# Second-level Strassen for M1 in the later quads of Mixer 2, with VectorE held in program order

## The chip, the core and the metric

The kernel runs on one core of one Trainium2 chip. The metric is device time in microseconds (us), taken over several executions. The four executions of the kernel before that stand beside the change agreed within 0.3 us (574.78 to 575.06).

Engines are named as the profile names them: PE is TensorE, DVE is VectorE, ACT is ScalarE, SP issues the transfers.

## The reference, cut to what matters

```python
h  = x + A(layernorm(x))                        # linear attention; A is not touched here
u  = gelu(einsum("bsd,sf->bdf", layernorm(layernorm(h)), w1) + b1)   # Mixer 1
y  = einsum("bdf,fs->bds", u, w2) + b2          # Mixer 2: 3584 -> 2048, 1024 columns
out = h + transpose(y)                          # residual
```

Only Mixer 2 is changed: a product of `w2` (3584 x 2048) with `u` (3584 x 1024), plus bias and residual `h`.

## The kernel before

Each pair of 128-row blocks of the output (512 columns a half) is one level of Strassen-Winograd: seven products instead of eight. The stationary operand is a block of `w2` or a sum of blocks; the moving operand is a block of `u` or a sum. I call the stationary sums by the number of the product that uses them, S5, S6, S7 and S3, and the moving sums T2, T3 and T4. The products accumulate in tiles A, B and C of PSUM, the memory that matmuls write to:

```python
def asum(self, m):                 # stationary sums, one DVE instruction each
    a, b, op = {
        5: (self.a21, self.a22, ALU.add),
        6: (self.lhs.get(5), self.a11, ALU.subtract),
        7: (self.a11, self.a21, ALU.subtract),
        3: (self.a12, self.lhs.get(6), ALU.subtract),
    }[m]
    t = pools["sa"].tile([P, self.nk, P], FP16, tag="sa", name="sa")[:]   # a pool of 6 buffers
    self.lhs[m] = t
    return nc.vector.tensor_tensor(t, a, b, op)
# p1: A = M1, ACT copies A to B    p6: B += M6, ACT copies B to C    p5: e = M5
# p2: A += M2 -> out(0,0)          p7: C += M7 -> out(1,1) = C + e
# p3: B += M3 -> out(0,1) = B + e  p4: C += M4 (needs T4) -> out(1,0)
```

Two pairs make a quad. In a quad the two M5 products together are again a 2 x 2 block product, and `Inner` does that one with Strassen too: seven products i1 to i7 of 256 columns. Mixer 1 already does so for M1 and M5; Mixer 2 does it for M5 only, in its quads 1, 2 and 3 (quad 0 is plain).

```python
def i1(self):
    ae = psz.tile([P, BANK], F32, tag="z0", bufs=1, name="psI0")
    bc = psz.tile([P, BANK], F32, tag="z1", bufs=1, name="psI1")
    self.a, self.e, self.b, self.c = ae[:, 0:HW], ae[:, HW:CW], bc[:, 0:HW], bc[:, HW:CW]
    self.mm(1, self.a, True)
    nc.scalar.copy(self.b, self.a)
# i6: b += ..., copy b to c   i2: a += ..., sink   i5: e = ..., copy e to SBUF
# i7: c += ..., c + e by DVE  i3: b += ..., b + e by DVE   i4: c += ..., sink
```

The order of a quad, cut to what matters. P4 of a quad runs inside the next quad, and while a quad runs, the next quad's sums are made (`pre`):

```python
for st in self.sts: st.p1()
for st in pend:     st.p4()          # P4 of the quad before, needs T4
on_p4()                              # T3, weight loads
interleave(self.in5, [st.p6 for st in self.sts])
pre(5)                               # next quad's S5 pair and inner sums
for st in self.sts: st.p2()
pre(6)                               # next quad's S6 pair
for st in self.sts: st.p7(...)
on_p7()                              # T4
pre(7)
for st in self.sts: st.p3()
pre(3)
```

The framework orders the instructions of each engine itself, by readiness in a model of the machine, with program order as the priority. An engine then executes its own list in that order.

## Time and profile before

| what | read from | value |
|---|---|---|
| time | median | 574.98 us |
| PE, DVE, ACT busy | page | 99%, 67%, 44% |
| one later quad (quad 2) | timeline of PE | 480.75 to 522.36, 41.61 us |
| 14 matmuls of 512 columns | timeline of PE | 3.02 us, 215.9 ns each |
| 7 matmuls of 256 columns | timeline of PE | 0.763 us, 109.0 ns each |
| DVE busy in such a quad | windows | about 27 of 41 us |

The prediction gives this quad as 480.91 to 522.52; that is the same stretch as the view of the chain places it.

First two lines of the page of the kernel before: busy time of each engine (us, share of the span, instructions), and the chain of work that ended last, by engine.

```profile
PE 566.0 (99%) x3061; PEld 287.2 (50%) x3061; DVE 383.8 (67%) x731; ACT 254.7 (44%) x547; POOL 1.8 (0%) x8
...
PE 93%; DVE 3%; DMA 2%; ACT 2%; issue 1%; SPq 0%; ACTq 0%
```

PE does nearly all of the chain. Next, the timeline of PE in the kernel before, some of quad 2. The columns are the start, the time from the first start to the last end, the engine, the line, the operation, output and inputs, shapes and the count; a bracket at the end would be idle time and what ended it. Busy spans of neighbours overlap (matmuls are pipelined), so lengths are read from start to start.

```profile
480.75 3.18 PE L285 MATMUL psA_5063<-gE,wq 128*128 128x512 f16 x14
483.77 3.19 PE L285 MATMUL psA_5080<-gE,wq 128*128 128x512 f16 x14
486.79 1.67 PE L285 MATMUL psC_4858<-gs_4997,wq 128*128 128x512 f16 x7
...
495.54 0.93 PE L218 MATMUL psI_5142<-gi_4451,is 128*128 128x256 f16 x7
496.31 0.93 PE L218 MATMUL psI_5141<-gE,sa 128*128 128x256 f16 x7
...
522.36 3.18 PE L285 MATMUL psA_5386<-gE,wq 128*128 128x512 f16 x14
```

There is no bracket anywhere in the 41.61 us: PE never waits. The two P1 (`psA`) take 6.04 us and need nothing that was made late, so the P4 behind them (`psC<-gs`, where `gs` holds T4) starts 6.04 us into the quad.

Last, the timeline of DVE of the same kernel at the end of the quad before.

```profile
471.88 1.09 DVE L277 TENSOR_TENSOR sa<-sa,wq 128x1792 f16<-128x1792 f16 x1 [2.27 <-PE psC_4858 L285]
472.89 0.74 DVE L395 SCALAR_TENSOR_TENSOR t_4973<-psC_4858,b_sb,e_4816 128x512 f32<-128x512 f32 x1
473.56 2.02 DVE L1241 TENSOR_TENSOR gs_4997<-gO,gT_4434 128x3584 f16<-128x3584 f16 x1
475.49 1.09 DVE L277 TENSOR_TENSOR sa<-sa,wq 128x1792 f16<-128x1792 f16 x1
```

The first line is the first S6 of the next quad. It waited 2.27 us for a buffer, until the first P7 had consumed its S7 (`psC` is P7's tile). The second S6 (last line) was not free yet, so the scheduler put half of T4 (`gs`) and a P7 eviction before it.

### The profile page before, as it was taken

How to read it: one execution, taken by the hardware profiler on the slowest of the kernel's cores; microseconds unless marked ns; L12 is line 12 of the kernel's file. 1: busy time of each engine (PE TensorE's matmuls, PEld its weight loads, DVE VectorE, ACT ScalarE, POOL GpSimd, SP SyncE). 2: the span in 40 equal slices, each digit the busy share in tenths (PEclk: the TensorE clock that was granted, in tenths of full speed). 3: DMA queues.
4: the chain of work that ended last, by engine and by line, in shares of the span. 5: the costliest groups of instructions: out<-in, count | busy, mean ns of one | idle time of the engine just before them, and what ended most of it. 6: DMA issues, size and time to landing. Idle time of an engine off the chain costs nothing.

```text
span 573.1 us, 8081 instructions
## 1 busy us (share of the span) xinstructions
PE 566.0 (99%) x3061; PEld 287.2 (50%) x3061; DVE 383.8 (67%) x731; ACT 254.7 (44%) x547; POOL 1.8 (0%) x8
## 2 busy tenths in 40 slices
PE   8999999999999999999999999999999999999997
PEld 3444444455555444446555565564444554544544
DVE  6898887556767879863745727442989558557535
ACT  5657777656667776445445354463110100100100
POOL 1000000000000000000000000000000000000000
PEclk9999999999999999999999999999999999999999
DMA  9934432039536762104041240425971852842001
GB/s 309 352 74 83 85 73 38 19 113 318 104 73 130 184 174 102 55 2 146 1 148 55 93 148 1 148 75 146 233 189 47 218 140 67 218 120 73 19 27 47
DMA packets 97798, 66.59 MB, mean 116 GB/s; under 512 B 32082, under 2 KB 91744, under 8 KB 97760
## 3 DMA queue, kind: packets, MB, share of 16 engines
q1 hardware_dynamic: 97024, 65.42, 41.7%
q10 hardware_dynamic: 672, 0.66, 0.3%
q8 instruction: 24, 0.39, 0.3%
q14 instruction: 14, 0.11, 0.1%
q0 software_dynamic: 64, 0.01, 0.0%
HBM read 50.34 MB, written 8.39 MB: 102 GB/s over the span
## 4 chain that ended last, share of the span: by engine, by line
PE 93%; DVE 3%; DMA 2%; ACT 2%; issue 1%; SPq 0%; ACTq 0%
PE acc_t L964 9%; PE acc_t L1112 9%; PE psB L695 4%; PE psC L695 4%; PE psA L695 4%; PE psE L695 2%; PE nd_ps L1063 1%; DMA xr<-in_A_x_dram 1%; PE psB_4758 L285 1%; PE psC_5500 L285 1%; PE psC_5181 L285 1%; PE psB_5064 L285 1%; PE psC_4858 L285 1%; PE psA_4757 L285 1%; PE psC_4527 L285 1%; PE psB_4550 L285 1%
## 5 line engine op out<-in xcount | busy, mean ns | idle before, releaser
L285 PEld LDWEIGHTS <-sa 128*128 128x128 f16 x716 | 70.0, 98 | 77.3 <-issue 0.7
L285 PEld LDWEIGHTS <-wq 128*128 128x128 bf16 x590 | 57.1, 98 | 61.7 <-issue 1.0
L964 PE MATMUL acc_t<-xnT,wq_sb 128*128 128x512 bf16 x256 | 58.0, 379 | 0.0
L1112 PE MATMUL acc_t<-wo_sb,pqT 128*128 128x512 bf16 x256 | 56.1, 379 | 0.0
L277 DVE TENSOR_TENSOR sa<-wq 128x1024 f16<-128x1024 bf16 (+1 forms) x44 | 36.4, 830 | 6.9 <-DMA wq<-in_B_w_dram 2.8
L1112 PEld LDWEIGHTS <-pqT 128*128 128x128 bf16 x256 | 24.8, 98 | 29.0
L964 PEld LDWEIGHTS <-wq_sb 128*128 128x128 bf16 x256 | 24.5, 98 | 27.4
L166 ACT ACTIVATE e_sb<-acc_t 128x512 bf16<-128x512 f32 x40 | 23.9, 597 | 26.5 <-PE acc_t L964 24.3
L170 DVE TENSOR_SCALAR e_sb<-e_sb 128x512 bf16<-128x512 bf16 x64 | 18.5, 289 | 25.4 <-ACT e_sb L166 24.8
L218 PEld LDWEIGHTS <-is 128*128 128x128 f16 x276 | 26.9, 98 | 14.3 <-issue 3.0
L695 PEld LDWEIGHTS <-xs 128*128 128x128 f16 x208 | 20.0, 98 | 23.3 <-DVE xs L681 1.3
L695 PE MATMUL psA<-wkv,xnT 128*128 128x512 bf16 x104 | 26.7, 379 | 0.0
L1123 DVE BATCH_NORM_STATS2 hst<-acc_t 128x6 f32<-128x512 f32 x32 | 22.1, 693 | 6.7 <-ACT h_bf L1122 6.5
L1110 ACT CAST acc_t<-xr 128x512 f32<-128x512 bf16 x32 | 19.0, 593 | 13.4 <-DVE hst L1123 13.3
L695 PEld LDWEIGHTS <-xnT 128*128 128x128 bf16 x156 | 15.3, 98 | 18.5 <-issue 0.2
L167 ACT ACTIVATE r_sb<-acc_t 128x512 bf16<-128x512 f32 x40 | 23.7, 593 | 0.0
L619 PE MATMUL acc_t<-wkv,xnT 128*128 128x512 bf16 x96 | 21.6, 379 | 0.7 <-ACT xnT L872 0.7
L1084 DVE TENSOR_TENSOR o_sb<-nd_ps,rd 128x384 bf16<-128x384 f32 (+1 forms) x48 | 21.7, 504 | 0.6 <-ACT rd L1079 0.4
L588 DVE BATCH_NORM_STATS2 st<-x_sb 128x6 f32<-128x512 bf16 x32 | 20.5, 681 | 1.6 <-DMA x_sb<-in_A_x_dram 1.6
L277 DVE TENSOR_TENSOR sa<-sa,wq 128x1024 f16<-128x1024 f16 (+1 forms) x22 | 18.3, 831 | 3.9 <-PE psC_4858 L285 2.3
L277 DVE TENSOR_TENSOR sa<-wq,sa 128x1024 f16<-128x1024 bf16 (+1 forms) x22 | 18.3, 831 | 3.7 <-PE psI_5141 L218 1.1
L1122 ACT CAST h_bf<-acc_t 128x512 bf16<-128x512 f32 x32 | 18.4, 575 | 1.0 <-PE acc_t L1112 0.9
(722 smaller groups left out, 979.1 us busy)
## 6 DMA issues: line engine op xcount, KB each, us to landing
wq<-in_B_w_dram SPq DMA_DIRECT2D x14, 1024.0 KB, 7.7
wq<-in_B_w_dram SPq DMA_DIRECT2D x8, 1792.0 KB, 10.0
xr<-in_A_x_dram SPq DMA_DIRECT2D x16, 256.0 KB, 3.1
out_dram<-ot SPq DMA_DIRECT2D x31, 128.0 KB, 1.7
x_sb<-in_A_x_dram SPq DMA_DIRECT2D x15, 256.0 KB, 3.2
wkv<-in_A_wqkv_dram SPq DMA_DIRECT2D x2, 1024.0 KB, 9.5
wq_sb<-in_A_wqkv_dram SPq DMA_DIRECT2D x2, 1024.0 KB, 12.7
wo_sb<-in_A_wo_dram SPq DMA_DIRECT2D x2, 1024.0 KB, 6.4
```

The lines of the kernel that those rows point to most:

```text
L166: pin(nc.scalar.activation(e_sb[:], src, ACT.Exp))
L167: pin(nc.scalar.activation(r_sb[:], src, ACT.Relu))
L218: nc.tensor.matmul(ps, lhsT=self.lhs[m][:, k, :], rhs=self.mov[m][:, k, :], start=(start and k == 0), stop=(k == self.nk - 1), skip_group_ ...
L277: return nc.vector.tensor_tensor(t, a, b, op)
L285: nc.tensor.matmul(ps[:, cols], lhsT=lhs[:, k, :], rhs=mv(k)[:, cols], start=(start and k == 0), stop=(k == self.nk - 1), skip_group_check ...
L588: return nc.vector.bn_stats(st[:, c, :], x_sb[:, c * CW:(c + 1) * CW])
L619: mm = nc.tensor.matmul(pp[:, 0:CW], lhsT=xnT[:, kt, i * P:(i + 1) * P], rhs=wkv[:, kt, c * CW:(c + 1) * CW], start=(kt == 0), stop=(kt == ...
L695: pin(nc.tensor.matmul(ps[:], lhsT=lhs[:, k, :], rhs=rhs[:, k, :], start=(start and k == 0), stop=(k == hk2 - 1), skip_group_check=True,))
L964: nc.tensor.matmul(qp[:, 0:SW], lhsT=wq_sb[:, kt, j * P:(j + 1) * P], rhs=xnT[:, kt, u * SW:(u + 1) * SW], start=(kt == 0), stop=(kt == ND ...
L1084: nc.vector.tensor_tensor(o_sb[:, b * JPB * P:(b * JPB + nsl) * P].rearrange("p (s h e) -> p s h e", h=HB, e=DH), blk[:, :, 0:P].rearrange ...
L1112: nc.tensor.matmul(ap_[:, 0:CW], lhsT=pqT[:, j, i * P:(i + 1) * P], rhs=wo_sb[:, j, dc * CW:(dc + 1) * CW], start=(j == 0 and not SEED_RES ...
L1123: nc.vector.bn_stats(st[:, dc, :], ap_[:, 0:CW])
```

## The change

The intent: M1 of quads 1 to 3 of Mixer 2 gets inner Strassen too, as in Mixer 1, which saves 1/8 of its matmul columns. Buffers and moving sums for it need room in SBUF (the on-chip memory of the operands), so the pool of the stationary sums shrinks from 6 to 4 (S7 is now made in place over a block of weights), and evictions move partly to ACT. From quad 1 on every DVE instruction is pinned behind the one traced before it (`dve.held`).

```diff
+    class Dve:
+        held = False
+        def __getattr__(self, name):
+            op = getattr(nc.vector, name)
+            return (lambda *a: pin(op(*a))) if self.held else op
 ... (class Mixer2)
+        def asum(self, m):
+            if m != 7:
+                return super().asum(m)
+            t = self.a21.bitcast(FP16)
+            self.lhs[7] = t
+            return dve.tensor_tensor(t, self.a11, self.a21, ALU.subtract)
 ...
         def out(self, sh, dh, a, b, op):
             op(ot[:, a:b], b2_sb[:, i:i + 1])
+            dve.tensor_tensor(ot[:, a:b], ot[:, a:b], self.hr[sh, dh][:, a:b], ALU.add)
 ...
         def evac(self, sh, dh, ps, a=0, b=CW):
-            self.out(sh, dh, a, b, lambda ot, bias: nc.vector.scalar_tensor_tensor(
-                ot, ps[:, a:b], bias, self.hr[sh, dh][:, a:b], ALU.add, ALU.add))
+            self.out(sh, dh, a, b, lambda ot, bias: nc.scalar.activation(
+                ot, ps[:, a:b], ACT.Identity, bias=bias, scale=1.0))
 ... (class Quad)
+        def begin2(self):
+            self.asums(5)
+            self.in1 = self.inner(1)
+            self.asums(6)
+        def run2(self, pend, nxt, on_p4, on_p7, cut):
+            ...
+            in5 = self.inner(5)
+            self.interleave(self.in1, [st.p4 for st in pend])
+            on_p4()
+            ...                                  # residual loads
+            self.asums(7)
+            self.interleave(in5, [st.p6 for st in sts])
+            self.asums(3)
+            ...                                  # p2, residual loads
+            nxt.begin2()                         # if there is a next quad
+            ...                                  # p7 of both pairs
+            on_p7()                              # T4
+            ...                                  # p3 of both pairs
+            return sts, nxt
 ... (Mixer 2 proper)
-    pools["sa"] = ctx.enter_context(tc.tile_pool(name="sapool2", bufs=6, ...))
+    pools["sa"] = ctx.enter_context(tc.tile_pool(name="sapool2", bufs=4, ...))
-    pools["is"] = inner2
+    pools["is"], pools["is_bufs"] = inner2, 7
+    mov1, sums1 = inner_moving(gE[:, :, 0:CW], NFP, inner2, "gi1")
 ... (end of quad 0)
+    dve.held = True
 ... (also cut: mends of T3, whose input is now overwritten; loads of the residual)
```

More of the change, by code (lines that the diff above doesn't have):

```diff
@@ L198, in inner_moving @@
         return {1: b11, 2: b21, 3: b22, 4: t4, 5: b12, 6: t2, 7: t3}, sums
+    class Dve:
[3 more added lines that the diff above has]
+            return (lambda *a: pin(op(*a))) if self.held else op
+    dve = Dve()
     class Inner:
@@ L208, in sums @@
         def sums(self):
-            sm = [pools["is"].tile([P, self.nk, P], FP16, tag=self.tag, bufs=4, name="is")[:] for _ in range(4)]
-            nc.vector.tensor_tensor(sm[0], self.a21, self.a22, ALU.add)
-            nc.vector.tensor_tensor(sm[1], sm[0], self.a11, ALU.subtract)
-            nc.vector.tensor_tensor(sm[2], self.a11, self.a21, ALU.subtract)
-            nc.vector.tensor_tensor(sm[3], self.a12, sm[1], ALU.subtract)
+            sm = [pools["is"].tile([P, self.nk, P], FP16, tag=self.tag, bufs=pools["is_bufs"], name="is")[:] for _ in range(4)]
+            dve.tensor_tensor(sm[0], self.a21, self.a22, ALU.add)
+            dve.tensor_tensor(sm[1], sm[0], self.a11, ALU.subtract)
+            dve.tensor_tensor(sm[2], self.a11, self.a21, ALU.subtract)
+            dve.tensor_tensor(sm[3], self.a12, sm[1], ALU.subtract)
             self.lhs.update({5: sm[0], 6: sm[1], 7: sm[2], 3: sm[3]})
@@ L276, in asum @@
             self.lhs[m] = t
-            return nc.vector.tensor_tensor(t, a, b, op)
+            return dve.tensor_tensor(t, a, b, op)
         def pre(self, m):
@@ L360, in evac_shared @@
         def evac_shared(self, fh, ps):
-            t = cpool.tile([P, BANK], F32, tag=f"t{fh}", name="t1")
+            t = pools["t"].tile([P, BANK], F32, tag=f"t{fh}", name="t1")
             nc.vector.tensor_tensor(t[:], ps[:], self.e[:], ALU.add)
@@ L371, in __init__, with fetch @@
             super().__init__(p, w2_tiles[p], NFP, gmov)
-        def prefetch(self):
             self.hr = {}
-            for sh in range(2):
-                for dh in range(2):
-                    t = outp.tile([P, CW], BF16, tag=f"hr{self.p % 2}{sh}{dh}", bufs=2 if (sh, dh) == (1, 0) else 1, name="hr")
-                    nc.sync.dma_start(t[:], h_dram[2 * self.p + sh][:, dh * CW:(dh + 1) * CW])
-                    self.hr[sh, dh] = t
+        def asum(self, m):
[4 more added lines that the diff above has]
+            return dve.tensor_tensor(t, self.a11, self.a21, ALU.subtract)
+        def fetch(self, sh, dh):
+            t = outp.tile([P, CW], BF16, tag="hr", bufs=6, name="hr")
+            nc.sync.dma_start(t[:], h_dram[2 * self.p + sh][:, dh * CW:(dh + 1) * CW])
+            self.hr[sh, dh] = t
         def out(self, sh, dh, a, b, op):
@@ L384, in out @@
             op(ot[:, a:b], b2_sb[:, i:i + 1])
+            dve.tensor_tensor(ot[:, a:b], ot[:, a:b], self.hr[sh, dh][:, a:b], ALU.add)
             nc.sync.dma_start(o_dram[i * P:(i + 1) * P, dh * CW + a:dh * CW + b], ot[:, a:b])
         def evac(self, sh, dh, ps, a=0, b=CW):
-            self.out(sh, dh, a, b, lambda ot, bias: nc.vector.scalar_tensor_tensor(
-                ot, ps[:, a:b], bias, self.hr[sh, dh][:, a:b], ALU.add, ALU.add))
+            self.out(sh, dh, a, b, lambda ot, bias: nc.scalar.activation(
+                ot, ps[:, a:b], ACT.Identity, bias=bias, scale=1.0))
         def evac_shared(self, sh, ps):
-            t = cpool.tile([P, BANK], F32, tag=f"t{sh}", name="t2")
-            def op(ot, bias):
-                nc.vector.scalar_tensor_tensor(t[:], ps[:], bias, self.e[:], ALU.add, ALU.add)
-                nc.vector.tensor_tensor(ot, t[:], self.hr[sh, 1][:], ALU.add)
-            self.out(sh, 1, 0, CW, op)
+            self.out(sh, 1, 0, CW, lambda ot, bias: dve.scalar_tensor_tensor(
+                ot, ps[:], bias, self.e[:], ALU.add, ALU.add))
         def done(self):
@@ L420, in sum1 @@
             A, B, c = self.sts[m].A, self.sts[m].B, self.cols(h)
-            nc.vector.tensor_tensor(A[:, c], ps, es, ALU.add)
+            dve.tensor_tensor(A[:, c], ps, es, ALU.add)
             nc.scalar.copy(B[:, c], A[:, c])
@@ L427, in sum5 @@
         def sum5(self, m, h, ps, es):
-            nc.vector.tensor_tensor(self.sts[m].e[:, self.cols(h)], ps, es, ALU.add)
+            dve.tensor_tensor(self.sts[m].e[:, self.cols(h)], ps, es, ALU.add)
         def pre(self, m):
@@ L438, in pre, with interleave, fill @@
                 self.in5.sums()
-        def prefetch(self):
-            for st in self.sts:
-                st.prefetch()
-        def run(self, pend, nxt, on_p4=nop, before_p7=nop, on_p7=nop, cut=None):
-            nk = self.sts[0].nk
-            def interleave(n, fs):
-                steps = [(f, k) for f in fs for k in range(nk)]
-                t = len(steps)
-                cuts = [0, (5 * t + 8) // 16, (9 * t + 8) // 16, (12 * t + 8) // 16, t]
-                def fill(q):
-                    part = steps[cuts[q]:cuts[q + 1]]
-                    for f in fs:
-                        ks = [k for g, k in part if g is f]
-                        if ks:
-                            f(ks)
-                for f in (n.i1, 0, n.i6, n.i2, 1, n.i5, n.i7, 2, n.i3, 3, n.i4):
-                    fill(f) if isinstance(f, int) else f()
+        def interleave(self, n, fs):
+            steps = [(f, k) for f in fs for k in range(self.sts[0].nk)]
+            t = len(steps)
+            cuts = [0, (5 * t + 8) // 16, (9 * t + 8) // 16, (12 * t + 8) // 16, t]
+            def fill(q):
+                part = steps[cuts[q]:cuts[q + 1]]
+                for f in fs:
+                    ks = [k for g, k in part if g is f]
+                    if ks:
+                        f(ks)
+            for f in (n.i1, 0, n.i6, n.i2, 1, n.i5, n.i7, 2, n.i3, 3, n.i4):
+                fill(f) if isinstance(f, int) else f()
@@ new lines, in asums, with inner @@
+        def asums(self, m):
+            for st in self.sts:
+                st.asum(m)
+        def inner(self, m):
+            mov, sink, sink_sum = {
+                1: (self.mov1, self.sink1, self.sum1), 5: (self.mov5, self.sink5, self.sum5),
+            }[m]
+            n = Inner(self.sts, m, mov, "i", sink, sink_sum)
+            n.sums()
+            return n
+        def begin2(self):
[3 more added lines that the diff above has]
+        def run2(self, pend, nxt, on_p4, on_p7, cut):
+            sts = self.sts
+            for st in sts:
+                st.begin()
+            in5 = self.inner(5)
+            self.interleave(self.in1, [st.p4 for st in pend])
+            on_p4()
+            for st in sts:
+                st.shared_tile()
+                st.fetch(0, 0)
+            for sh, dh in ((1, 1), (0, 1)):
+                for st in sts:
+                    st.fetch(sh, dh)
+            self.asums(7)
+            self.interleave(in5, [st.p6 for st in sts])
+            self.asums(3)
+            nxt = nxt()
+            for st in sts:
+                st.p2()
+            for st in sts:
+                st.fetch(1, 0)
+            if nxt is not None:
+                nxt.begin2()
+            for st in sts:
+                st.p7(cut if st is sts[-1] else None)
+            on_p7()
+            for st in sts:
+                st.p3()
+            return sts, nxt
@@ L462, in run @@
+        def run(self, pend, nxt, on_p4=nop, before_p7=nop, on_p7=nop, cut=None):
+            interleave = self.interleave
             if self.mov1 is not None:
@@ L1187 @@
     cpool = ctx.enter_context(tc.tile_pool(name="cpool", bufs=1))
+    pools["t"] = mctx.enter_context(tc.tile_pool(name="tpool", bufs=1, side="right"))
     assert NFP % 2 == 0 and NSP % 2 == 0 and NSP >= 4 and NFP >= 6
     inner1 = mctx.enter_context(tc.tile_pool(name="inner1", bufs=1, side="right"))
-    pools["is"] = inner1
+    pools["is"], pools["is_bufs"] = inner1, 4
     hmov.update(moving(hE, hO, hT2, hT3, hT4))
@@ L1218 @@
     mctx.close()
-    pools["sa"] = ctx.enter_context(tc.tile_pool(name="sapool2", bufs=6, side="right", reuse_waits="tile"))
+    pools["sa"] = ctx.enter_context(tc.tile_pool(name="sapool2", bufs=4, side="right", reuse_waits="tile"))
     w2b = ctx.enter_context(tc.tile_pool(name="w2b", bufs=2, side="right", reuse_waits="tile"))
@@ L1235, with derived @@
     gmov.update(moving(gE, gO, gT2, None, None))
-    def derived(m, of):
+    def derived(m, of, mend=None):
         def make():
@@ L1240, in make, with less_b11 @@
             for h, sl in enumerate(spans):
-                nc.vector.tensor_tensor(ts[h][:], *of(sl), ALU.subtract)
+                dve.tensor_tensor(ts[h][:], *of(sl), ALU.subtract)
+                if mend is not None:
+                    mend(ts[h], sl)
             gmov[m] = lambda k: ts[k // H2][:, k % H2, :]
         return make
-    make_t3 = derived(7, lambda sl: (gT2[:, sl, :], gE[:, sl, 0:CW]))
+    def less_b11(t, sl):
+        k0 = sl.start + sl.start % 2
+        o = t[:, k0 - sl.start:H2:2, HW:CW]
+        dve.tensor_tensor(o, o, gE[:, k0:sl.stop:2, 0:HW], ALU.subtract)
+    make_t3_raw = derived(7, lambda sl: (gT2[:, sl, :], gE[:, sl, 0:CW]))
+    make_t3 = derived(7, lambda sl: (gT2[:, sl, :], gE[:, sl, 0:CW]), less_b11)
     make_t4 = derived(4, lambda sl: (gO[:, sl, 0:CW], gT2[:, sl, :]))
@@ L1249 @@
         load_w2(p, w2b)
+    mov1, sums1 = inner_moving(gE[:, :, 0:CW], NFP, inner2, "gi1")
     mov5, sums5 = inner_moving(gE[:, :, CW:D], NFP, inner2, "gi5")
     def quad2(u):
-        return Quad([Mixer2(2 * u), Mixer2(2 * u + 1)], None, mov5)
+        return Quad([Mixer2(2 * u), Mixer2(2 * u + 1)], mov1, mov5)
     def after_p4(u):
@@ L1265 @@
     for st in pend:
-        st.prefetch()
+        st.fetch(0, 0)
+        st.fetch(1, 1)
+        st.fetch(0, 1)
+    for st in pend:
         if st is pend[1]:
-            for m in (5, 6, 7, 3):
+            for m in (5, 6, 7):
                 st.asum(m)
-            make_t3()
+            make_t3_raw()
         st.p1()
@@ L1274 @@
         st.p6()
+        if st is pend[1]:
+            st.asum(3)
+    sums1()
     sums5()
-    nxt.pre(5)
+    for st in pend:
+        st.fetch(1, 0)
+    nxt.begin2()
     for st in pend:
@@ L1279 @@
     make_t4()
-    nxt.pre(6)
-    nxt.pre(7)
     for st in pend:
         st.p3()
-    nxt.pre(3)
+    dve.held = True
     for u in range(1, NSP // 2):
         cur = nxt
-        cur.prefetch()
         last = 2 * u + 2 == NSP
-        pend, nxt = cur.run(
-            pend, lambda: None if last else quad2(u + 1),
-            on_p4=after_p4(u), on_p7=make_t4, cut=CW - P if last else None,
+        pend, nxt = cur.run2(
+            pend, lambda: None if last else quad2(u + 1), after_p4(u), make_t4, CW - P if last else None,
         )
```

## The prediction

> **What bounds the kernel now.** TensorE. The page gives PE 99% busy, VectorE (DVE) 67%, ScalarE (ACT) 44%; the chain of waits is 93% PE. In Mixer 2 (403 to 570 us) the timeline shows matmul groups back to back: 14 matmuls of 512 columns every 3.02 us (215.9 ns each), 7 of 256 columns every 0.763 us (109.0 ns). That agrees with the Trainium skill ("TensorE: Matmul & The Clock Gate", Back-to-back issue gap: N/2.4 + 2.5 ns). A later quad takes 41.61 us (480.91 to 522.52) with no PE gap. Only fewer matmul columns help.
>
> **Removed.** Inner Strassen replaces 28 x 215.9 ns = 6.05 us of M1 by 49 x 109.0 ns = 5.34 us: 0.71 us per quad, three quads, 2.1 us, all on the critical path.
>
> **Added, off PE.** Per later quad, DVE gets four more inner sums (0.62 us each), two mends of T3 (estimate 0.5 each) and two partial sums (0.42). A residual add with fp32 input took 0.69 us, an all-16-bit one of 512 columns takes 0.42; the fused (0,0) and (1,0) evictions (0.75) move to ACT, leaving a 0.42 add. DVE goes from about 27 to about 30 us of a 41 us quad (estimate). Quad 0 also gets four M1 moving sums (1.09 each); DVE is nearly full there, with slack after 444 us. ACT is nearly idle. Capacity suffices everywhere.
>
> **Moved, where I expect the gain to go.** DVE now runs in program order (the skill's table at the head of the TensorE page lists VectorE's queue as strict FIFO, so a blocked instruction blocks those behind). The sum pool shrinks from 6 to 4. While a quad's S3 pair lives and the next quad's S5 pair is made, all four are taken, so the next quad's S6 pair must wait for P3 of the current quad, its last product. S6 stands in DVE order *before* the P7 evictions and the T4 sums. Before, DVE slipped T4 ahead of a blocked sum; now it cannot. At the end of P3 (time 0) DVE still owes: S6 1.0, two P7 evictions 2.3, T4 2 x 2.0, two P3 evictions 2.3, four in5 sums 2.3, then the first M1 partial sum near 12.7 us (estimate). P4 cannot start before about 5.3.
>
> The scheduler does reorder PE (in Mixer 1 some inner groups swap), so I expect PE to run most of in1 (4.6 us) first, with about 0.5 us exposed behind the ACT copy after i1, and 0.9 us or more before i4, which needs that partial sum: 1.5 to 2.2 us per transition. It happens between quads 1 and 2 and 2 and 3 only (quad 0 is not held, quad 3 has no successor): about 3 to 4.4 us. If PE kept program order, P4 would stall about 4.5 us each time. The last eviction becomes ACT then DVE: about 0.2 us.
>
> **Sum.** 575.0 - 2.1 + 3 + 0.2 = about 576, say 575.9 us; 80% range 572.6 to 580.5. Chances: faster by over 2% 0.01, within 2% 0.97, slower 0.02.
>
> **What would show it.** Inner M1 groups of 7 matmuls at 0.763 us: step 1 right. S6 (128x1792) in DVE's timeline released by P3's psB at the end of quads 1 and 2, the P7 evictions queued after it: blocking right. PE gaps of 0.5 to 5 us at the starts of quads 2 and 3, released by DVE: cost right. No such gaps and a span near 571: wrong.
>
> **What would make it wrong.** The late T4 fully hidden behind in1; an order of PE or ACT that waits on what DVE does last; quad 0's fuller DVE delaying quad 1; late residual or weight loads.

## The result, and the profile after

The changed kernel takes 579.14 us (median of 4 runs, 578.94 to 579.27) against 574.91 us (4 runs) for the kernel before: ratio 1.0069, 95% interval 1.0054 to 1.0084. It is slower by 4.2 us, where its matmul work is 2.1 us less.

The same two lines of the page, of the changed kernel:

```profile
PE 565.5 (98%) x3124; PEld 293.5 (51%) x3124; DVE 390.2 (68%) x759; ACT 272.0 (47%) x585; POOL 1.8 (0%) x8
...
PE 90%; DVE 6%; issue 1%; ACT 1%; DMA 1%; SPq 0%; DVEq 0%; ACTq 0%
```

The shares barely move. What moved is the chain: DVE's part of it doubles from 3% to 6%. The timeline of PE, read from start to start of the quads, says where:

| | before | after | difference |
|---|---|---|---|
| quad 1 | 41.61 (439.14 to 480.75) | 40.92 (439.27 to 480.19) | -0.69 |
| quad 2 | 41.61 (480.75 to 522.36) | 43.61 (480.19 to 523.80) | +2.00 |
| quad 3 | 41.61 (522.36 to 563.97) | 43.61 (523.80 to 567.41) | +2.00 |
| from there to the end of the span | 9.13 (to 573.1) | 9.99 (to 577.4) | +0.86 |

With 0.13 us of difference before quad 1, these sum to the 4.3 us between the spans (573.1 and 577.4). Quad 1 is what the change was made for: 0.69 us gained. Quads 2 and 3 have the same matmuls, so they lose 43.61 - 40.92 = 2.69 us each to waits.

The timeline of PE in the changed kernel around the start of quad 2, beginning with P7 and P3 of quad 1 (`psI` are the inner products, `psC<-gs,wq` from 485.84 is P4). I call the inner products of M1 and M5 together in1 and in5, as the code does:

```profile
468.10 6.21 PE L294 MATMUL psC<-gs,wq 128*128 128x512 f16 x28
474.14 6.21 PE L294 MATMUL psB<-gO,sa 128*128 128x512 f16 x28
480.19 0.93 PE L227 MATMUL psI<-gE,wq 128*128 128x256 f16 x7
481.61 0.93 PE L227 MATMUL psI<-gi,is 128*128 128x256 f16 x7 [0.50 <-ACT psI L237]
482.37 0.93 PE L227 MATMUL psI<-gE,wq 128*128 128x256 f16 x7
483.14 0.60 PE L227 MATMUL psI<-gi,is 128*128 128x256 f16 x4
483.80 0.92 PE L227 MATMUL psI<-gE,is 128*128 128x256 f16 x7
484.56 0.49 PE L227 MATMUL psI<-gi,is 128*128 128x256 f16 x3
485.19 0.81 PE L227 MATMUL psI<-gE,sa 128*128 128x256 f16 x6
485.84 6.21 PE L294 MATMUL psC<-gs,wq 128*128 128x512 f16 x28
491.88 0.27 PE L227 MATMUL psI<-gE,sa 128*128 128x256 f16 x1
492.83 0.93 PE L227 MATMUL psI<-gE,is 128*128 128x256 f16 x7 [0.68 <-DVE psA L205]
494.28 0.92 PE L227 MATMUL psI<-gi,wq 128*128 128x256 f16 x7 [0.52 <-DVE psA L205]
```

In program order P4 is interleaved with i1 to i7. Here the scheduler has run i1, i6, i2, i7 and i5 and even the first product of in5, because P4 was not ready. From start to start, less 109.0 ns a matmul, PE loses 0.66 us before i6, 0.22 before i5, 0.30 before in5's i1, 0.84 before i3 (at 492.83) and 0.69 before i4 (at 494.28), together 2.71. The first three follow ACT copies that P4's matmuls would have covered; the last two follow DVE's M1 partial sums (`psA`).

The timeline of DVE in the changed kernel, same stretch:

```profile
477.37 1.09 DVE L205 TENSOR_TENSOR sa<-sa,wq 128x1792 f16<-128x1792 f16 x1 [3.65 <-PE psB L294]
480.39 1.09 DVE L205 TENSOR_TENSOR sa<-sa,wq 128x1792 f16<-128x1792 f16 x1 [1.93 <-PE psB L294]
481.40 0.74 DVE L205 SCALAR_TENSOR_TENSOR ot<-psC,b_sb,e 128x512 bf16<-128x512 f32 x1
...
483.64 3.95 DVE L205 TENSOR_TENSOR gs<-gO,gT 128x3584 f16<-128x3584 f16 x2
...
491.48 0.62 DVE L205 TENSOR_TENSOR is<-sa,is 128x896 f16<-128x896 f16 x1
...
492.35 0.43 DVE L205 TENSOR_TENSOR psA<-psI,es 128x256 f32<-128x256 f32 x1
493.79 0.43 DVE L205 TENSOR_TENSOR psA<-psI,es 128x256 f32<-128x256 f32 x1 [1.01 <-PE psI L227]
```

The two S6 now wait for `psB`, which is P3, the last product of the quad: 3.65 and 1.93 us of a standing engine. The first P7 eviction stands behind them and starts at 481.40, though both P7 products were complete by 474.31 (468.10 plus 6.21). T4 follows at 483.64, the first M1 partial sum at 492.35, which is 12.2 us after the quad's start. DVE worked 29 us in this quad and still was late with what counted.

The reader should set this beside the same place before: there the second S6 was also blocked, and the scheduler passed it with T4. The change also took cover away. Before, P4 came 6.04 us into the quad, behind P1; now it is to start behind i1, 0.77 us into the quad (s6_last_b below). The first half of T4, late as it is, was ready 5.47 us into quad 2 (483.64 plus 2.02, the time of one half in the kernel before), so by these numbers P1 would still have covered it. That was not run.

### The profile page after: what moved, and what is told of

The parts are those of the page before. It is cut to its first block, busy times and chain, and to the rows that moved or that the text cites. A ratio compares the mean times of both kernels' runs of the same rounds, so it can differ in the third digit from the quotient of the medians.

```text
span 577.4 us, 8298 instructions
## 1 busy us (share of the span) xinstructions
PE 565.5 (98%) x3124; PEld 293.5 (51%) x3124; DVE 390.2 (68%) x759; ACT 272.0 (47%) x585; POOL 1.8 (0%) x8
## 4 chain that ended last, share of the span: by engine, by line
PE 90%; DVE 6%; issue 1%; ACT 1%; DMA 1%; SPq 0%; DVEq 0%; ACTq 0%
PE psB L294 17%; PE psC L294 15%; PE psI L227 11%; PE psA L294 10%; PE acc_t L1016 9%; PE acc_t L1164 9%; PE psB L747 4%; PE psC L747 4%; PE psA L747 4%; PE acc_t L671 2%; PE psE L747 2%; PE psE L294 1%; DVE gs L205 1%; PE nd_ps L1115 1%; DVE ot L205 1%
## 5 line engine op out<-in xcount | busy, mean ns | idle before, releaser
L294 PEld LDWEIGHTS <-wq 128*128 128x128 bf16 (+1 forms) x618 | 59.9, 98 | 63.7 <-issue 1.0
L294 PE MATMUL psC<-gs,wq 128*128 128x512 f16 (+2 forms) x238 | 50.2, 366 | 0.0
L330 ACT COPY psC<-psB 128x512 f32<-128x512 f32 x22 | 12.5, 570 | 35.1 <-PE psB L294 35.1
L294 PE MATMUL psB<-hT,sa 128*128 128x512 f16 x112 | 28.4, 379 | 0.0
L294 PE MATMUL psC<-hT,wq 128*128 128x512 f16 x112 | 28.3, 379 | 0.0
L205 DVE TENSOR_TENSOR ot<-ot,hr 128x512 bf16<-128x512 bf16 (+2 forms) x27 | 11.2, 414 | 24.8 <-ACT ot L403 24.4
L294 PE MATMUL psB<-gT,sa 128*128 128x512 f16 x112 | 26.5, 379 | 0.0
L294 PE MATMUL psA<-hO,wq 128*128 128x512 f16 x112 | 25.6, 379 | 0.7 <-ACT psB L313 0.7
L294 PE MATMUL psB<-hO,sa 128*128 128x512 f16 x112 | 25.5, 379 | 0.0
L294 PE MATMUL psC<-hT,sa 128*128 128x512 f16 x112 | 25.5, 379 | 0.0
```

The costliest lines, as they stand in the source:

```text
L205: return (lambda *a: pin(op(*a))) if self.held else op
L294: nc.tensor.matmul(ps[:, cols], lhsT=lhs[:, k, :], rhs=mv(k)[:, cols], start=(start and k == 0), stop=(k == self.nk - 1), skip_group_check ...
L330: nc.scalar.copy(self.C[:], self.B[:])
```

## The experiments

Theory: the S6 pair has no buffer until P3 is done; it stands in a fixed DVE order before the P7 evictions and T4; so these start 7 us or more late, P4 cannot cover the copies between the inner products, and the M1 partial sums come too late. What DVE still has to do when P3 ends is called the debt below.

Rivals: DVE has simply too much work at the transition; the fixed order as such costs the time; the in5 sums in front of the partial sums are what counts.

| run | edit | median us | ratio to before (95%) |
|---|---|---|---|
| the change | | 579.14 | 1.0069 (1.0054 to 1.0084) |
| s6_last | S6 after the P3 evictions | 573.29 | 0.9977 (0.9962 to 0.9992) |
| s6_last_b | the same, 5 rounds | 573.18 | 0.9969 (0.9957 to 0.9982) |
| s6_mid | S6 after the P7 evictions | 575.23 | 1.0003 (0.9990 to 1.0017) |
| bufs5 | 5 sum buffers, 2 output tiles | 580.18 | 1.0083 (1.0069 to 1.0097) |
| bufs5b | 5 sum buffers, 3 output tiles | 574.96 | 1.0000 (0.9985 to 1.0015) |
| in5_late | in5 sums later | 578.08 | 1.0054 (1.0039 to 1.0069) |
| before_held | the kernel before, DVE held | 575.93 | 1.0025 (1.0008 to 1.0041) |
| unheld | the change, DVE free | 585.49 | 1.0184 (1.0148 to 1.0219) |
| pin_in1 | unheld, only the M1 inner sums pinned | 574.84 | 0.9996 (0.9982 to 1.0009) |
| s6_last_tail | s6_last, last evictions on DVE | 572.93 | 0.9963 (0.9949 to 0.9976) |

### s6_last: the same work, another place in the queue

```diff
 def begin2(self):
     self.asums(5)
     self.in1 = self.inner(1)
-    self.asums(6)
 ... (run2; likewise at the end of quad 0)
     for st in sts:
         st.p3()
+    if nxt is not None:
+        nxt.asums(6)
     return sts, nxt
```

> The changed kernel with one move: the next quad's S6 pair is made after the P3 evictions in VectorE order, no longer before the P7 evictions. Theory (a blocked S6 pair at the head of the in-order VectorE holds up the P7 evictions and T4): the S6 pair still waits for P3, but nothing that TensorE needs soon stands behind it; quads 2 and 3 shrink from 43.61 us to 40.9 each, time about 573.8 us (579.1 minus 2 x 2.7). Rival (VectorE simply has too much work at the transition, or the fixed order as such costs it): the amount of work and the hold are unchanged, so at most 1 us is won and the time stays above 578.

Measured: 573.29 us, and 573.18 in the repeat: 0.5 us below the expected 573.8. The transitions give 2 x 2.7 us back; the rest is probably in the last stores (see s6_last_tail). In the first run one of the four executions, the profiled one, took 575.01: its quads are 40.91 to 40.92 us as well, but it lost 1.7 us in its first 12 us, where PE ran slower. So it was repeated for a clean profile.

> s6_last once more, with five rounds, to set it beside s6_last_tail (572.93) and to take a profile of an execution whose clock was up from the start: 573.2 to 573.4 us, quads of 40.9 us, the last stores landing in 1.6 and 1.5 us.

The timelines of DVE and of PE in s6_last_b, the same place:

```profile
473.55 0.74 DVE L205 SCALAR_TENSOR_TENSOR ot<-psC,b_sb,e 128x512 bf16<-128x512 f32 x1
...
475.79 3.95 DVE L205 TENSOR_TENSOR gs<-gO,gT 128x3584 f16<-128x3584 f16 x2
...
481.90 2.08 DVE L205 TENSOR_TENSOR sa<-sa,wq 128x1792 f16<-128x1792 f16 x2
```

```profile
480.10 0.93 PE L227 MATMUL psI<-gE,wq 128*128 128x256 f16 x7
480.87 2.11 PE L294 MATMUL psC<-gs,wq 128*128 128x512 f16 x9
482.81 0.93 PE L227 MATMUL psI<-gi,is 128*128 128x256 f16 x7
```

T4 is made at 475.79 instead of 483.64, P4 interleaves with the inner products as the program has it, and PE shows no wait at all: quads 1 and 2 start at 439.19 and 480.10, quad 3 at 521.02, 40.9 us each. The number of DVE instructions is the same (759), so "too much work" falls, and so does "the fixed order as such": it is still fixed.

### s6_mid: half the move

```diff
     for st in sts:
         st.p7(cut if st is sts[-1] else None)
+    if nxt is not None:
+        nxt.asums(6)
     on_p7()
```

(and S6 taken out of `begin2`, as above.)

> A half step of the move in s6_last: the S6 pair behind the P7 evictions (2.3 us of VectorE), still before T4 and the P3 evictions. Theory: the debt at the end of P3 is 2.3 us smaller, so the first M1 partial sum comes about 10 us after the quad's start instead of 12.2. TensorE then no longer waits for it (1.5 us of 2.7 gone), but T4 is still late, so i6 still waits for the ACT copy after i1: 1.0 to 1.3 us lost per transition, time 575.5 to 576.5. Rival (only full removal helps, or it is not a queue): near 579 or near 573.3.

Measured: 575.23 us, 0.3 below the range. Quad 2 takes 41.91 us (479.97 to 521.88 in the timeline of PE), so 1.0 us is lost instead of 2.69. The only wait of PE that the profile names is the one of 0.50 us behind the ACT copy, once in each of the two transitions; it names none for the partial sums. A trace of one is left: before i3 PE loses 0.21 us, and i3 starts at 490.37, 0.05 us after the first partial sum ends (489.89 plus 0.43). The loss follows the length of the debt, as a queue should.

### bufs5 and bufs5b: one buffer more, the same order

```diff
-name="sapool2", bufs=4
+name="sapool2", bufs=5
-pools["is"], pools["is_bufs"] = inner2, 7
+pools["is"], pools["is_bufs"] = inner2, 6      # bufs5b: 5
-ot = outp.tile([P, CW], BF16, tag="ot", bufs=3, name="ot")
+ot = outp.tile([P, CW], BF16, tag="ot", bufs=2, name="ot")   # bufs5 only
```

> The changed kernel in its own order, with 5 buffers for the sums instead of 4 (the room comes from 6 inner-sum buffers instead of 7 and 2 output tiles instead of 3). Theory (the missing buffer makes S6 wait for P3): one S6 finds a free buffer, the other needs only the first P3, 3.0 us earlier. So the S6 wait in VectorE is released at P3's first product, T4 is ready some 2.4 us after the quad's start, and 0.5 to 1.2 us are lost per transition instead of 2.7: 574.8 to 576.5. Rival (S6 waits for something else, its place alone counts): 579.

Measured: 580.18 us, a miss: slower than the change. Three lines of its timelines, ACT, DVE and PE in turn, show another queue.

```profile
496.81 0.69 ACT L403 ACTIVATE ot<-psC,b_sb 128x512 bf16<-128x512 f32 x1 [3.00 <-DMA out_dram<-ot]
```

```profile
497.52 0.43 DVE L205 TENSOR_TENSOR ot<-ot,hr 128x512 bf16<-128x512 bf16 x1 [6.46 <-ACT ot L403]
```

```profile
505.53 1.43 PE L227 MATMUL psI<-gE,is 128*128 128x256 f16 x7 [3.23 <-DVE e L205]
```

With two output tiles, the ACT eviction of P4 waited for an earlier store, which had been issued among weight loads. DVE, in its fixed order, waited 6.46 us for that eviction with T3 and the M5 partial sums behind it, and PE then waited 3.23 us. That is the price of the room I had taken, not of the fifth buffer, so the run was mended.

> bufs5 again without its flaw: the fifth buffer for the sums is paid for by inner-sum buffers alone (5 instead of 7), and the three output tiles are kept, since in bufs5 an output tile waiting for a store behind a weight load stalled ACT, then VectorE in its order, then TensorE for 3.2 us. Theory (the missing buffer makes S6 wait for the last product): the first half of the pair waits for nothing, the second for the first P3; 0.7 to 1.3 us lost per transition, no wait of TensorE over 0.7 us, 575.0 to 576.5 us. Rival (the buffer is not what S6 waits for): 579.

Measured: 574.96 us, at the lower edge of the range. The timeline of DVE in bufs5b:

```profile
473.48 1.08 DVE L205 TENSOR_TENSOR sa<-sa,wq 128x1792 f16<-128x1792 f16 x1
477.21 1.09 DVE L205 TENSOR_TENSOR sa<-sa,wq 128x1792 f16<-128x1792 f16 x1 [2.65 <-PE psB L294]
478.22 0.75 DVE L205 SCALAR_TENSOR_TENSOR ot<-psC,b_sb,e 128x512 bf16<-128x512 f32 x1
```

The first S6 waits for nothing; the second starts at 477.21, when the first P3 is done, instead of 480.39. Everything behind it is 3.2 us earlier, and quad 2 takes 41.81 us. So it is the buffer that S6 waits for. (No run has six buffers with this order.)

### in5_late: is it the sums in front of the partial sums?

```diff
-            in5 = self.inner(5)
             self.interleave(self.in1, [st.p4 for st in pend])
+            in5 = self.inner(5)
```

> The changed kernel with the four in5 sums (2.3 us of VectorE) moved behind the M1 partial sums and the P4 residual adds. The two later waits of TensorE at a transition (0.68 and 0.52 us named, 0.84 and 0.69 with the gaps) end with the M1 partial sums, which stand behind these sums. If they end the queue that counts: each quad 0.8 to 1.5 us shorter, 576.2 to 577.5 us. The wait behind the ACT copy after i1 (0.5 us) must stay, since the late T4 is not touched. Rival (the in5 sums are harmless): 579.1.

Measured: 578.08 us, outside the range: a miss. Quads 2 and 3 take 42.92 us (quad 2 from 481.02 to 523.94), so 0.7 us came back in each. The 0.50 us wait stayed, and the sums, now late themselves, made new waits of up to 0.63 us for the M5 partial sums in all three quads; quad 1 grew by 0.8 us, to 41.72 (439.30 to 481.02). Of the 1.06 us won, about 0.6 is that of the last stores, which landed in 1.6 and 1.5 us here (see s6_last_tail). The in5 sums were part of the debt, but moving them only moves it.

### before_held: what the fixed order costs by itself

```diff
     nxt.pre(3)
+    dve.held = True
     for u in range(1, NSP // 2):
```

(with the `Dve` helper of the change used in place of `nc.vector` in Mixer 2.)

> The kernel before, with VectorE in program order from quad 1 on and nothing else. There the S6 pair waits for P7 (pool of 6), not for P3, and P1 of the next quad gives 6 us of cover before P4 needs T4. Theory: the hold as such costs nothing, 574.5 to 575.5 us. Rival (the hold as such costs): 2 us or more above 574.9.

Measured: 575.93 us (one of the four executions took 577.53), 0.9 over the kernel before, neither the theory's nothing nor the rival's 2 us. The quads take 41.91 us instead of 41.61; small gaps stand around the last inner products, none of them large enough for the profile to list as a wait. So the order as such has a price of 0.3 us a quad in that kernel, a ninth of what a quad of the change loses.

### unheld and pin_in1: why the order was held at all

```diff
-    dve.held = True
```

> The changed kernel with VectorE left to the scheduler (no hold), S6 left where it was and the pool of 4. Theory: the scheduler slips the P7 evictions and T4 ahead of the blocked S6 pair as it did in the kernel before, and most of the 2 x 2.7 us comes back: 573.5 to 575.5 us. Rival (too much VectorE work, hold or not): about 579. If it gets slower than 579, the scheduler's free order has another cost, which the hold was there to avoid.

Measured: 585.49 us (582.93 to 588.39), the third of the three outcomes. The late T4 is indeed gone: quads 2 and 3 start with P4 interleaved and no wait. Two lines of DVE and four of PE in unheld show what came instead:

```profile
462.30 0.63 DVE L219 TENSOR_TENSOR is<-wq 128x896 f16<-128x896 bf16 x1 [4.91 <-DMA wq<-in_B_w_dram]
...
463.50 0.42 DVE L438 TENSOR_TENSOR e<-psI,es 128x256 f32<-128x256 f32 x1
```

```profile
463.97 1.65 PE L227 MATMUL psI<-gE,is 128*128 128x256 f16 x7 [4.79 <-DVE e L438]
465.42 3.19 PE L294 MATMUL psB<-gT,sa 128*128 128x512 f16 x7
...
510.33 1.65 PE L227 MATMUL psI<-gE,is 128*128 128x256 f16 x7 [2.55 <-DVE e L438]
511.78 2.51 PE L294 MATMUL psB<-gT,sa 128*128 128x512 f16 x7
```

The scheduler put an inner sum of the *next* quad, which needs weights that were still in flight, ahead of the M5 partial sum that PE needed. DVE stood 4.91 us for the transfer and PE 4.79 us with it. Left alone, PE also came back slow: the seven matmuls start at 463.97 and the group after them at 465.42, 207 ns a matmul instead of 109, and the granted clock from 463.9 to 468.4 us is 0.50. The Trainium skill ("TensorE: Matmul & The Clock Gate", The two states you'll see) has the clock halve after an idle window of about 3.4 us. The 4.79 us wait fits that, but the second such wait of this run does not: it took 2.55 us, and the matmuls after it start 207 ns apart too, at a granted clock of 0.50 (510.3 to 511.8 us). So here less idle time was enough, and the measurement decides. The two waits cost 7.3 us; the slow matmuls after them cost about 4.0 us more (an estimate: from 463.97 to 469.50 and from 510.33 to 514.88, less the times at full speed).

To see whether that one inversion is all that is wrong with the free order, only these sums were pinned:

```diff
-            self.in1 = self.inner(1)
+            dve.held = True
+            self.in1 = self.inner(1)
+            dve.held = False
```

> The unheld kernel with one thing held: the four M1 inner sums of the next quad stay behind the sums traced before them. In unheld the first of them stood at the head of VectorE waiting 4.9 us for the weight load, ahead of the M5 partial sum that TensorE needed. Theory: with that order alone mended, the scheduler's free order lets T4 pass the blocked S6 and no wait of TensorE over 0.7 us is left: 573 to 575 us. Rival (free order is bad in general): above 579.

Measured: 574.84 us, between 573.80 and 575.67. In the profiled execution, the fastest, PE shows no wait and the quads take 41.15 to 41.17 us. So the inversion was the cause, and a free DVE passes the blocked S6. One of the four runs had a clock of 0.997; what spreads the other three over 1.6 us is open.

### s6_last_tail: the end of the kernel

```diff
         def evac(self, sh, dh, ps, a=0, b=CW):
+            if self.p >= NSP - 2 and (sh, dh) == (1, 0):
+                return self.out(sh, dh, a, b, lambda ot, bias: dve.scalar_tensor_tensor(
+                    ot, ps[:, a:b], bias, self.hr[sh, dh][:, a:b], ALU.add, ALU.add), True)
```

(`True` leaves the separate residual add out.)

> s6_last, with the last pair's (1,0) evictions fused on VectorE again as in the kernel before, instead of ACT and then VectorE. Theory: the ACT step stands on the tail after the last matmul; 0.3 us shorter to the last VectorE instruction, and up to 0.6 us more if the slower landing of the last stores (2.3 and 2.0 us instead of 1.6 and 1.5) came with it: 572.3 to 573.0 us. Rival (the tail is set by the stores, not the evictions): 573.3.

Measured: 572.93 us, ratio 0.9963 (0.9949 to 0.9976), against 573.18 us and 0.9969 for s6_last_b; the two were sent apart, and the intervals overlap. The profiles show the term itself: from the start of the last P4 to the end of the span 9.15 us here (561.75 to 570.9), as in the kernel before (9.13), and 9.4 with the ACT step (s6_mid: 563.80 to 573.2). So about 0.3 us of the tail is the extra step. The other 0.58 us of the change's 0.86 comes after the last DVE instruction (3.08 us to the end of the span, 2.50 in the kernel before): it is its last two stores, which landed in 2.3 and 2.0 us there and in 1.6 and 1.5 in before, s6_last and s6_mid. A packet of the instruction queue fell among them in that one profile; whether it is the cause was not tested. All four executions of the change took about as long (578.94 to 579.27), so the slow stores were probably in each of them.

This version is 2.0 us faster than the kernel before and 6.2 us faster than the change.

## Why the prediction was right or wrong

The measured 579.14 us lies in the predicted range of 572.6 to 580.5 and within 2% as forecast; the point, 575.9, was 3.2 us too low: 2.4 of it for the transitions and 0.7 for the tail. The range is so wide that it also holds s6_last (573.29), where PE waits for nothing, so the hit by itself says little for the mechanism. The profile and the runs do.

- **What M1 saves: right.** 0.71 us a quad predicted; 0.69 in quad 1 of the change, and 2.0 us in all once nothing gives it back (s6_last_tail against the kernel before).
- **Capacity suffices: right.** DVE was to go from 27 to about 30 us of a quad. It is 29.0 of 40.9 us in quad 1 of s6_last_b, where PE never waits. The mends of T3 took 0.69 and 0.56 us for the estimated 0.5.
- **The blocked S6: right**, including what released it (P3), the order behind it, and that quad 1 is spared. Removing the place (s6_last), shortening the debt (s6_mid) and adding the buffer (bufs5b) each remove what they should, or a little more.
- **The size of a transition: the term that was mis-sized.** "1.5 to 2.2 us per transition" measured 2.69, and the sum then took 3 us for two, the low end of its own "3 to 4.4", where they cost 5.4. The clock times of the debt were good: P4 at 5.65 us (5.3 predicted), the first partial sum at 12.2 (12.7). What was missing is on PE's side. I let i3 run before any partial sum, since it writes half b of its tile and the sum reads half c. But both halves lie in one PSUM bank, and i3 started 0.05 us after the sum's end: it waited 0.84 us, and i4 then waited 0.69 for the second sum. The Trainium skill ("PSUM — Partial Sum Buffer", Terms, PSUM bank) calls PE and another engine at the same bank at once a collision, so such a wait has to be there; in s6_mid, too, i3 starts 0.05 us after that sum ends. That it is the bank and not only the shared tile was not tested apart. The other missing part is 0.5 us for two more ACT copies that P4 would have covered; I had counted only the one after i1 (0.5 predicted, 0.66 measured).
- **The tail: mis-sized.** 0.2 us predicted, 0.86 measured: 0.3 for the ACT step, the rest the stores.

The terms add up: s6_last_b at 573.18, plus 2 x 2.69, plus 0.58 of slow stores, is 579.14.

## What to carry to other kernels

An in-order engine at 68% busy can still be the one that everything waits for: ask of each instruction in its queue what it waits for, and who stands behind it. When a pool is shrunk, count which buffers are live at each allocation; the first instruction without a free one moves to the end of some consumer, and in a fixed order it takes all that follows along. Pinning is not the fault by itself: fully pinned, the kernel took 579.14 us with S6 in the wrong place and 573.18 in the right one; free but for the scheduler's one mistake it took 574.84, and wholly free 585.49. Place work that is bound to be blocked after what the critical engine needs next.

## What the Trainium skill lacked or had wrong

- "TensorE: Matmul & The Clock Gate", Back-to-back issue gap: it gives about 131 ns a matmul as the sustained rate of LDWEIGHTS and MATMUL pairs at 512 columns, and says that N/2.4 + 2.5 over-counts there. In these traces, with a weight load for every matmul, 14 matmuls of 512 columns take 3.02 us, 215.9 ns each, and 7 of 256 columns 0.763 us, 109.0 each. The formula holds; the 131 ns is not seen.
- The same page, table at its head: it lists VectorE's queue as strict FIFO, but no page that I read puts a price on a blocked head. Here it cost 2.69 us a quad with DVE 68% busy over the kernel, and 4.79 and 2.55 us in unheld.
- "PSUM — Partial Sum Buffer", Terms: bank sharing is given as an error to avoid. What it costs where a wait keeps the two engines apart is not given: here probably 0.84 us, for a matmul group whose half of the tile nobody was reading (the bank and the shared tile were not tested apart).
- No page that I read says that a pool with too few output tiles makes stores queued among weight loads hold up compute: 6.46 us of DVE and 3.23 us of PE in bufs5.
